# One group of four PSUM buffers for table fills, K generator, DFT steps and transposes of x

## The chip, the core and the metric

The kernel runs on one core of a Trainium2 chip. The metric is the time of one execution in microseconds (us) on the device. A time of the kernel is the median of several runs; the profile is of one further execution.

Engines are called by the names of the profile: PE multiplies matrices (PEld loads its weights), ACT evaluates functions and copies, DVE does elementwise work and copies, POOL sets constants and issues a few transfers, SP issues most transfers. PE writes only into PSUM, which has eight banks of 2 KB for each of its 128 partitions. What PE leaves there has to be copied out ("evicted") by ACT or DVE before the buffer can be filled again.

## The reference, cut to what matters

Two independent halves share the launch: part A, a local attention with 32 heads over x, and part B, a long convolution of u with a kernel K that is generated from parameters.

```python
# part A: qkv = x @ wqkv; each position attends to 8 positions at distance 0, 2, ..., 14
# x (1, 2048, 640), wqkv (640, 1920), wo (640, 640); H = 32, Dh = 20
logits = jnp.einsum("bhsd,bhswd->bhsw", q, kg) * scale
attn = softmax(logits)
a = einsum("bhsw,bhswd->bhsd", attn, vg) -> (1, 2048, 640) @ wo
# part B: u (1, 2048, 640), parameters (640, 192)
P = jnp.exp(logdA[:, :, None] * l[None, None, :])       # l = 0 .. 2047
K = jnp.einsum("dn,dnl,dn->dl", Cc, P, dB).real         # 640 channels x 2048
y = irfft(rfft(K padded) * rfft(u padded))[:2048] + u * Dskip
return concatenate([a, y], axis=-1)
```

## The kernel before, in words

**Part B** works on five chunks (`NCH`) of 128 channels, each in two halves (`th` = 0, 1). A half makes a table of exponentials times sines and cosines, from which the K generator multiplies out K.

- `table_steps` (L185) returns 18 steps for a half. Each takes a PSUM buffer of two banks (`new`, L209), fills it on PE by `block` (L201: matmul lines L203 and L206) and evicts it on ACT: one step for `E` (L216, Exp), three for `M` (L224, Exp), two for `MX` (L238, Exp), twelve for the sines of `Y` and `X` (L252, Sin). Between Exp and Sin, ACT loads a function table. The sines come in three blocks; after the second sine of `Y` in a block DVE does L258, L259 and L260, after the second of `X` it does L264. `M`, `MX` and `E` have one buffer each in SBUF: the next half's L224 waits for this half's L260, L238 for L264.
- `kgen_steps` (L274) is the K generator of a half: 256 small matmuls. L290 reads the first two blocks of `X` and `Y`, L294 reads the third. `jp` = 0 and 1 are two groups of eight channels with one PSUM bank each; each is evicted by one ACT copy (L297) into `Ksb`.
- `fwd_steps` (L366) is a DFT in two rounds of four steps: `f1` (L381, eviction into `A`) and `f2` (L392, eviction into `Ssp`). Every `f2` step reads what all four `f1` steps left in `A`. It is done for u (with `WU`, stored to DRAM as `Udram`) and for K (with `WK`); after each `f2` of K comes a product with the spectrum of u on DVE (`prod`, L420). `inv_steps` holds the first inverse round (`ia`, L429, eviction into `Z`, stored as `Zdram`).
- `Evac` (L337; its copies stand at L342) deals evictions out to engines by a pattern: "d" is DVE, "a" is ACT. For u and `ia` it is "da"; for K it is "d" for `f1` and "aad" for `f2`, and in the last chunk "da" and "a".

`partB` (L437) interleaves the 18 fills of the next half with a list `work`: the K generator of the half just filled, and then either the `ia` steps of the chunk before and the DFT of u of the chunk after next (while `th` = 1 is filled), or the DFT of K of this chunk with its products (while the next chunk's `th` = 0 is filled). In the last chunk `att.transposes` (L628) takes the place of the DFT of u: it transposes x on PE (L637) in 12 steps, evicted into `xa` and `xb`. Then come the projections of q and k (L657), interleaved with what is left of part B, and part A goes on to its products (L713).

PSUM is divided by tags. Before the change: tag "tb", two buffers of two banks, for table fills; tag "k", two buffers of one bank, for the K generator, later for the projections; tag "w", one buffer of two banks, for everything else (`f1`, `f2`, `ia`, transposes). In the last chunk the DFT steps take turns between "w" and "tb".

The order in which instructions stand on each engine is not written out by hand: a scheduler places them at build time, by program order, by what is ready and by free buffers in its own reckoning. Each engine then runs its list strictly in order; a waiting instruction holds up all that stand behind it on its engine. ACT's fills, and in the first chunk some copies, are kept in program order by `InOrder` (L28), so that there are few table loads. SP's queue is also in order.

Of the kernel before, what the change touches and what calls it, by code (L numbers as in the profile page):

```python
# [14 lines left out]
f32 = mybir.dt.float32  # L15
# [22 lines left out]
def params_src(prm):  # L38

    names = ["B_B_re", "B_B_im", "B_C_re", "B_C_im", "B_A_re", "B_A_im"]  # L40
    views = [prm[nm].rearrange("(g c t) n -> c g t n", g=4, c=NCH, t=32) for nm in names]
    return lambda a, c: views[a][c]
# [100 lines left out]
def new_pieces(tc, pools):  # L143


    nc = tc.nc
    PF = pools["arena"].tile([128, 8, CW], f16, name="PF", tag="PF", bufs=2)
    PM = pools["arena"].tile([128, 8, CW], f16, name="PM", tag="PM", bufs=2)
    nc.gpsimd.memset(PF[32:64], 0.0)
    nc.gpsimd.memset(PF[32:33], 4096.0)  # L150
    nc.gpsimd.memset(PM[64:128], 0.0)
    return PF, PM


def load_pieces(tc, P, scr, c, parts, sorder=lambda x: None):
    nc = tc.nc
    PF, PM = P
    where = {0: [(1, PM, 0), (4, PM, 1), (0, PF, 0), (3, PF, 1), (2, PF, 4), (5, PF, 5)], 1: [(6, PM, 2), (7, PM, 3)], 2: [(8, PF, 6), (9, PF, 7)]}
    for p in parts:
        for k, t, r in where[p]:  # L160
            sorder(nc.sync.dma_start(out=t[16 * r:16 * r + 16], in_=scr[c, k].rearrange("(g t) n -> t g n", t=16)))
# [23 lines left out]
def table_steps(tc, pools, R, P, th, order, Y, X, rows=(128, 128), vorder=None):  # L185
# [4 lines left out]
    nc = tc.nc  # L190
# [4 lines left out]
    pool, psp = pools["arena"], pools["psum"]  # L195
# [11 lines left out]
                   tile_position=(0, 64 * h), skip_group_check=True)  # L207

    def new():  # L209
        return psp.tile([128, 2, 512], f32, name="ps_t", tag="tb", bufs=2)  # L210

    def gens():
        ps = new()
        for blk in range(6):
            block(ps[:, 0, 32 * blk:32 * blk + 32], blk, PM, RM[:, 768:800], rows[0])
        order(nc.scalar.activation(out=E[:].rearrange("p k (b q) t -> p b k (q t)", b=6), in_=ps[:, 0, 0:192].rearrange("p (b k t) -> p b k t", k=2, t=16), func=ACT.Exp))  # L216
# [57 lines left out]
def kgen_steps(tc, pools, th, Y, X, Ksb):  # L274
    nc = tc.nc
    MM = nc.tensor.matmul
    st = {}

    def part(jp, half, k0):
        def run():  # L280
            if half == 0 and k0 == 0:
                st[jp] = pools["psum"].tile([128, 8, 64], f32, name="ps_k", tag="k", bufs=2)
            ps = st[jp]
            for k in range(k0, k0 + 4):
                t = 8 * jp + k
                for r in range(2):
                    for g in range(4):
                        o = ps[32 * g:32 * g + 32, k, :]
                        if half == 0:
                            MM(o, lhsT=X[:, r, 4 * g + t // 4, :, t % 4], rhs=Y[:, r, 4 * g + t // 4, :, t % 4], start=(k == 0 and r == 0), stop=False, tile_position=(0, 32 * g), skip_group_check=True)  # L290
                        else:
                            hb = 64 * (g // 2)
                            kq = 4 * (4 + g % 2) + t // 4
                            MM(o, lhsT=X[hb:hb + 64, r, kq, :, t % 4], rhs=Y[hb:hb + 64, r, kq, :, t % 4], start=False, stop=(r == 1),  # L294
                               tile_position=(hb, 32 * g), skip_group_check=True)
            if half == 1 and k0 == 4:
                nc.scalar.copy(out=Ksb[:, 16 * th + 8 * jp:16 * th + 8 * jp + 8], in_=ps[:])  # L297
        return run
    return [part(jp, half, k0) for jp in range(2) for half in range(2) for k0 in (0, 4)]


def fft_consts_np():
# [44 lines left out]
def interleave(a, b):  # L347
    na, nb = len(a), len(b)
    ia = ib = 0
    while ia < na or ib < nb:  # L350
        if ib >= nb or (ia < na and ia * nb <= ib * na):
            a[ia](); ia += 1
        else:
            b[ib](); ib += 1
# [47 lines left out]
def inv_steps(tc, pools, IA, Ud, banks, ev, done):  # L402


    nc = tc.nc
    pool = pools["arena"]
    MM = nc.tensor.matmul
    st = {}

    def load():  # L410
        U = st["U"] = pool.tile([128, 2, 4, 32, 32], bf16, name="U", tag="U")
        fl = lambda t: t.rearrange("p g k t -> p (g k t)")
        nc.sync.dma_start(out=fl(U[:, 0]), in_=Ud)
        for h in range(2):
            nc.sync.dma_start(out=fl(U[64 * h:64 * h + 64, 1]), in_=Ud[64 - 64 * h:128 - 64 * h])

    def prod(S, q):
        ks = slice(8 * q, 8 * q + 8)
        u = st["U"][:, :, :, ks]
        nc.vector.tensor_tensor(out=u, in0=u, in1=S[:, :, ks].unsqueeze(1).to_broadcast([128, 2, 4, 8, 32]), op=A.mult)  # L420

    def ia(q):
        def run():
            if q == 0:
                st["Z"] = pool.tile([128, 128, 32], bf16, name="Z", tag="Z")[:]
            ps = banks("ps_ia")
            for i in range(8):
                for r in range(2):
                    MM(ps[:, i], lhsT=st["U"][:, r, :, :, 8 * q + i].rearrange("p g k -> p (g k)"), rhs=IA[:, r], start=(i % 4 == 0 and r == 0), stop=(r == 1), skip_group_check=True)  # L429
            ev(st["Z"][:, :, 8 * q:8 * q + 8], ps[:].rearrange("p t m -> p m t"))  # L430
            if q == 3:
                done(st["Z"])
        return run
    return load, prod, [ia(q) for q in range(4)]


def partB(tc, pools, prm, B_u, B_Dskip, out_b, att):  # L437
    nc = tc.nc
# [3 lines left out]
    with ExitStack() as outer:  # L442
# [1 line left out]
        Ud = dpool.tile([NCH, 128, 4096], bf16, name="Udram")  # L444
        Zd = dpool.tile([NCH, 128, 4096], bf16, name="Zdram")
        scr = dpool.tile([NCH, 10, 128, CW], f16, name="scr")
        psk = outer.enter_context(tc.tile_pool(name="psum_k", bufs=2, space=bass.MemoryType.PSUM))
        ar = pools["arena"]
        pools.update(psum=psk)
        order, vorder, sorder = InOrder(tc), InOrder(tc), InOrder(tc)  # L450
        tiny = ar.tile([128, 1], f32, name="tiny")
        nc.vector.memset(tiny[:], 1e-36)
        pools["tiny"] = tiny
        tags = [("w", 1)]
        psrc = params_src(prm)
        last = NCH - 1
        ev = Evac(nc, "da")
# [59 lines left out]
        def u_steps(c, ev=ev):  # L517
            return fwd_steps(tc, pools, BD, WU, (lambda t: u[:, :, 32 * c + t]), Banks(psk, tags), ev, ev,
                             done=(lambda S: nc.sync.dma_start(out=Ud[c], in_=S[:].rearrange("p g k t -> p (g k t)"))))
        work = u_steps(0, Evac(nc, "da", dict(a=order, d=vorder)))  # L520
# [8 lines left out]
        for c in range(NCH):  # L529
            Ksb = ar.tile([128, 32, 64], bf16, name="Ksb", tag="Ksb", bufs=2)  # L530
            if c:
                P = nextP
            tg = tags if c < last else [("w", 1), ("tb", 2), ("tb", 2)]
            done = lambda Z, c=c: nc.sync.dma_start(out=Zd[c], in_=Z.rearrange("p m t -> p (m t)"))
            load, prod, ia = inv_steps(tc, pools, IA, Ud[c], Banks(psk, tg), evz, done)
            for th in range(2):
                if c or th:
                    interleave(table_steps(tc, pools, (RF, RM), P, th, order, Yb[th], Xb[th]), work)
                work = kgen_steps(tc, pools, th, Yb[th], Xb[th], Ksb)
                if th == 0:  # L540
                    work += prev_ia if c else []
                    if c + 2 < NCH:
                        work += u_steps(c + 2)
                    elif c + 2 == NCH:
                        work.append(lambda: nc.vector.tensor_tensor(out=u[:], in0=u[:], in1=Dsb[:].unsqueeze(1).to_broadcast([128, 64, 160]), op=A.mult))
                    else:
                        att.load_x()
                        work += att.transposes(lambda: psk.tile([128, 2, 512], f32, name="ps_xt", tag="w", bufs=1))
                    if c < last:
                        nextP = new_pieces(tc, pools)  # L550
                        load_pieces(tc, nextP, scr, c + 1, (0, 1, 2))
                else:
                    load()
                    e2 = Evac(nc, "aad") if c < last else Evac(nc, "a")
                    work += fwd_steps(tc, pools, BD, WK, (lambda t, Ksb=Ksb: Ksb[:, t, :]), Banks(psk, tg), Evac(nc, "d" if c < last else "da"), e2, each=prod)
            prev_ia = ia
        for st in work[:8]:
            st()
        att.load_w()
        kbank = lambda: psk.tile([128, 512], f32, name="ps_qk", tag="k", bufs=2)  # L560
        evh = Evac(nc, "a")
        interleave(work[8:] + prev_ia, att.proj_k(0, kbank, evh) + att.proj_q(0, kbank, evh))
    psa = pools["open_psum_a"]()
# [269 lines left out]
def kernel(  # L833
# [26 lines left out]
    pools["open_psum_a"] = lambda: ctx.enter_context(tc.tile_pool(name="psum_a", bufs=8, space=bass.MemoryType.PSUM))  # L860
    att = Attention(tc, pools, A_x, A_wqkv, A_wo, out_a)
    partB(tc, pools, prm, B_u, B_Dskip, out_b, att)


# [28 lines left out]
```

## Time and profile before

| what | us |
|---|---|
| median of 3 runs (lowest, highest) | 539.57 (536.38, 543.05) |
| the profiled execution's own time | 537.3 |
| span of the profiled execution, first to last instruction | 535.5 |
| PE, DVE, ACT busy, of the span | 396.6, 388.8, 345.6 |

The profiled execution has 1.8 us around its span, and lies 2.27 us below the median.

How to read it: each row of a group has the source line, the engine and operation, the tile written and the tiles read, partitions and elements, how often, the busy time and the mean of one. "Idle before" is how long the engine stood still before these instructions, and the arrow names what ended the wait; "issue" means that the profile shows nothing that it waited for. Rows of the timeline begin with their start in the span. Rows of the stretches begin with the stretch and its length, then busy time and count for PE, PEld, DVE, ACT and POOL, the granted share of PE's clock, the share of the transfer engines and GB/s.

The stages can be told by the first L224 of each half on ACT. They start at 79.2, 119.9, 149.8, 175.5, 205.5, 231.2, 258.6, 282.0 and 315.1 us. These nine stretches are called H1 to H9 here; odd ones fill `th` = 1, even ones `th` = 0 of the next chunk. H1 still contains the preparation of four chunks' parameters on DVE and ACT. After H9's fills come the projections, and at 384.0 us the first product of part A (L713).

### The profile page before, as it was taken

Reading aid. Unit: us, or ns where it says so; the run is one execution under the profiler, and the core shown is the slowest. Engines: PE = TensorE matmul, PEld = TensorE weight load, DVE = VectorE, ACT = ScalarE, POOL = GpSimd, SP = SyncE. Lnnn points to the kernel's source line nnn. Section 1 sums busy time; section 2 is a strip of 40 time slices with the busy share of each in tenths; the row PEclk is TensorE's granted clock in tenths of the full one; section 3 lists DMA queues with packets and bytes.
Section 4 is the critical chain, followed back from the end, with each engine's and each line's share of the span. In section 5 each row is a group of like instructions: output and inputs, shape, how many; then the busy total and the mean of one; then the engine's idle time right before and its main releaser. Section 6 shows DMA issues by size and latency. Waiting matters only on the chain. (4 is left out here: it accounts for less than half of the span.)

```text
span 535.5 us, 15509 instructions
## 1 busy us (share of the span) xinstructions
PE 396.6 (74%) x7009; PEld 253.5 (47%) x7009; DVE 388.8 (73%) x420; ACT 345.6 (65%) x461; POOL 35.5 (7%) x51
## 2 busy tenths in 40 slices
PE   0143778578778967887886787599799797877787
PEld 0012446344556646664554464455444474545345
DVE  3645598795979597989892988434485999985940
ACT  2393486598788987979896869357445273643254
POOL 8700001020012001200000000000000000000000
PEclk9999998598899999999999989999989799776989
DMA  4497133336006400444007008902102003653513
GB/s 123 107 160 190 54 112 121 96 136 138 1 17 190 127 24 18 135 118 148 4 14 225 2 4 287 268 2 80 80 1 62 1 4 82 217 101 109 121 64 111
DMA packets 51706, 51.57 MB, mean 96 GB/s; under 512 B 37416, under 2 KB 48360, under 8 KB 48696
## 3 DMA queue, kind: packets, MB, share of 16 engines
q1 hardware_dynamic: 49752, 49.69, 34.2%
q0 software_dynamic: 1184, 0.89, 0.8%
q8 instruction: 55, 0.90, 0.7%
q10 hardware_dynamic: 704, 0.00, 0.1%
q14 instruction: 11, 0.09, 0.1%
HBM read 32.30 MB, written 18.19 MB: 94 GB/s over the span
## 5 line engine op out<-in xcount | busy, mean ns | idle before, releaser
L252 ACT ACTIVATE X<-ps_t 128x1024 bf16<-128x1024 int16 x60 | 60.2, 1050 | 3.2 <-PE ps_t L203 2.1
L252 ACT ACTIVATE Y<-ps_t 128x1024 bf16<-128x1024 int16 x60 | 59.5, 1040 | 1.7 <-PE ps_t L206 0.9
L203 PE MATMUL ps_t<-R,PF 128*128 128x512 f16 (+1 forms) x160 | 52.3, 422 | 7.1 <-ACT Y L252 3.8
L772 DVE TENSOR_TENSOR prod<-v,attn 128x2048 bf16<-128x2048 bf16 (+1 forms) x48 | 47.6, 1041 | 12.8 <-PE ps_o L776 12.7
L203 PE MATMUL ps_t<-R,PM 128*128 128x256 f16 (+3 forms) x160 | 23.4, 266 | 37.9 <-DMA PM<-scr 23.6
L342 DVE CAST A<-ps_f 128x1024 bf16<-128x1024 f32 x28 | 34.2, 1221 | 23.7 <-PE ps_f L381 23.7
L713 DVE TENSOR_TENSOR prod<-qT,kT 128x5120 bf16<-128x5120 bf16 x16 | 44.6, 2818 | 8.9 <-ACT qT L342 4.7
L342 ACT CAST Ssp<-ps_f 128x1024 bf16<-128x1024 f32 x26 | 26.5, 1020 | 27.5 <-PE ps_f L392 23.9
L258 DVE TENSOR_TENSOR Y<-Y,M 128x2048 bf16<-128x2048 bf16 x30 | 36.6, 1218 | 6.9 <-ACT Y L252 6.9
L260 DVE TENSOR_TENSOR Y<-Y,M 128x2048 bf16<-128x2048 bf16 x30 | 36.6, 1220 | 0.3
L264 DVE TENSOR_TENSOR X<-X,MX 128x2048 bf16<-128x2048 bf16 x30 | 36.6, 1219 | 0.4 <-ACT X L252 0.2
L381 PE MATMUL ps_f<-BD,u 128*64 128x128 bf16 x320 | 22.6, 296 | 17.8 <-DMA BD<-c_BD 6.8
L290 PE MATMUL ps_k<-Y,X 128*32 128x64 bf16 x1280 | 31.4, 240 | 4.8 <-issue 2.8
L203 PEld LDWEIGHTS <-PM 128*128 128x128 f16 (+1 forms) x160 | 13.3, 101 | 44.7 <-DMA PM<-scr 23.6
L776 PE MATMUL ps_o<-prod,ident 32*32 32x512 bf16 (+1 forms) x768 | 23.6, 392 | 13.8 <-DVE prod L772 11.3
L294 PE MATMUL ps_k<-Y,X 64*32 64x64 bf16 x1280 | 27.7, 234 | 5.4 <-issue 3.8
L224 ACT ACTIVATE M<-ps_t 128x1024 bf16<-128x1024 f32 x30 | 29.5, 1033 | 3.3 <-DVE Y L260 1.9
L206 PE MATMUL ps_t<-R,PF 128*64 128x512 f16 (+1 forms) x160 | 26.4, 388 | 6.8 <-ACT Y L252 4.0
L381 PEld LDWEIGHTS <-u 128*64 128x64 bf16 x320 | 21.2, 203 | 21.6 <-issue 20.9
L290 PEld LDWEIGHTS <-X 128*32 128x32 bf16 x1280 | 22.7, 118 | 17.3 <-issue 10.4
L420 DVE TENSOR_TENSOR U<-U,Ssp 128x2048 bf16<-128x2048 bf16 x20 | 23.9, 1221 | 7.3 <-ACT Ssp L342 7.3
L429 PE MATMUL ps_ia<-IA,U 128*128 128x128 bf16 x320 | 25.3, 227 | 4.7 <-DVE Z L342 3.7
(146 smaller groups left out, 794.8 us busy)
## 6 DMA issues: line engine op xcount, KB each, us to landing
Udram<-Ssp SPq DMA_DIRECT2D x5, 1024.0 KB
U<-Udram SPq DMA_DIRECT2D x5, 1024.0 KB
U<-Udram SPq DMA_DIRECT2D x10, 512.0 KB
Zdram<-Z SPq DMA_DIRECT2D x5, 1024.0 KB
zq<-Zdram SPq DMA_DIRECT2D x25, 192.0 KB
u<-in_B_u_dram SPq DMA_DIRECT2D x4, 640.0 KB
xn<-in_A_x_dram SPq DMA_DIRECT2D x4, 640.0 KB
out_dram<-ob SPq DMA_DIRECT2D x16, 160.0 KB
```

The costliest lines, as they stand in the source:

```text
L203: MM(ps, lhsT=Pt[0:K, 2 * blk + th, 0:128], rhs=rhs[0:K], start=True, stop=True, skip_group_check=True)
L224: order(nc.scalar.activation(out=M[:].rearrange("p (q y) -> p q y", q=2)[:, :, 1024 * b:1024 * b + 1024].rearrange("p q (k z) -> p q k z", ...
L252: order(nc.scalar.activation(out=dst, in_=ps[:].bitcast(i16)[:, :, 0::2].rearrange("p i (k z) -> p (i k) z", z=128), func=ACT.Sin, scale=S ...
L258: V.tensor_tensor(out=hi, in0=lo, in1=m(0), op=A.mult)
L260: V.tensor_tensor(out=lo, in0=lo, in1=m(1), op=A.mult)
L264: V.tensor_tensor(out=xf, in0=xf, in1=mx, op=A.mult)
L290: MM(o, lhsT=X[:, r, 4 * g + t // 4, :, t % 4], rhs=Y[:, r, 4 * g + t // 4, :, t % 4], start=(k == 0 and r == 0), stop=False, tile_positio ...
L294: MM(o, lhsT=X[hb:hb + 64, r, kq, :, t % 4], rhs=Y[hb:hb + 64, r, kq, :, t % 4], start=False, stop=(r == 1), tile_position=(hb, 32 * g), s ...
L342: ins = self.nc.scalar.copy(out=out, in_=in_) if e == "a" else self.nc.vector.tensor_copy(out=out, in_=in_)
L381: MM(ps[64 * r:64 * r + 64, i], lhsT=src_fn(8 * q + i), rhs=BD[:, r], start=(i % 4 == 0), stop=True, skip_group_check=True, tile_position= ...
L713: self.nc.vector.tensor_tensor(out=pr[:], in0=self.qT[:, hf], in1=self.kT[:, hf, :, :, HALO - DIL * w:HALO - DIL * w + 256], op=A.mult)
L772: nc.vector.tensor_tensor(out=p2[:, 0:nd], in0=self.v2[b][:, :, off:off + 256], in1=self.attn[:, hf, w, :].unsqueeze(1).to_broadcast([128, ...
```

## The change: what it does

All users of PSUM in part B draw from one tag "b" with four buffers of two banks. The K generator takes one of these for all sixteen channels of a half instead of two of one bank for eight channels each; its eight steps run over both groups of channels for the first two blocks first, then over both for the third, and one ACT copy of 128x1024 takes the place of two of 128x512. The last chunk's DFT has the same four buffers as all others, and so have the transposes and the first projections (which use one bank of each).

```diff
     def new():
-        return psp.tile([128, 2, 512], f32, name="ps_t", tag="tb", bufs=2)
+        return psp.tile([128, 2, 512], f32, name="ps_t", tag="b", bufs=4)
...
-            if half == 0 and k0 == 0:
-                st[jp] = pools["psum"].tile([128, 8, 64], f32, name="ps_k", tag="k", bufs=2)
-            ps = st[jp]
+            if jp == half == k0 == 0:
+                st[0] = pools["psum"].tile([128, 16, 64], f32, name="ps_k", tag="b", bufs=4)
+            ps = st[0]
             for k in range(k0, k0 + 4):
                 t = 8 * jp + k
                 for r in range(2):
                     for g in range(4):
-                        o = ps[32 * g:32 * g + 32, k, :]
+                        o = ps[32 * g:32 * g + 32, t, :]
...
-            if half == 1 and k0 == 4:
-                nc.scalar.copy(out=Ksb[:, 16 * th + 8 * jp:16 * th + 8 * jp + 8], in_=ps[:])
+            if jp == half == 1 and k0 == 4:
+                nc.scalar.copy(out=Ksb[:, 16 * th:16 * th + 16], in_=ps[:])
         return run
-    return [part(jp, half, k0) for jp in range(2) for half in range(2) for k0 in (0, 4)]
+    return [part(jp, half, k0) for half in range(2) for jp in range(2) for k0 in (0, 4)]
...
-        psk = outer.enter_context(tc.tile_pool(name="psum_k", bufs=2, space=bass.MemoryType.PSUM))
+        psk = outer.enter_context(tc.tile_pool(name="psum_k", bufs=4, space=bass.MemoryType.PSUM))
...
-        tags = [("w", 1)]
+        tags = [("b", 4)]
...
-            tg = tags if c < last else [("w", 1), ("tb", 2), ("tb", 2)]
+            tg = tags
...
-                        work += att.transposes(lambda: psk.tile([128, 2, 512], f32, name="ps_xt", tag="w", bufs=1))
+                        work += att.transposes(lambda: psk.tile([128, 2, 512], f32, name="ps_xt", tag="b", bufs=4))
...
-        kbank = lambda: psk.tile([128, 512], f32, name="ps_qk", tag="k", bufs=2)
+        kbank = lambda: psk.tile([128, 512], f32, name="ps_qk", tag="b", bufs=4)
```

The changed program has the same instructions on PE. On ACT, 10 copies take the place of 20. The scheduler's order differs over most of part B: in the built program of the changed kernel PE takes fills and DFT steps in turn, and the DFT steps of a half are done before the next half's fills begin; before, several of them stood between or behind the next half's fills.

## Prediction

> **What bounds the kernel now.** I read the page's busy times first, then the busy times by stretch, then the timelines of PE, ACT and DVE in the stretches that stand still longest.
>
> ```profile
> span 535.5 us, 15509 instructions
> ...
> PE 396.6 (74%) x7009; PEld 253.5 (47%) x7009; DVE 388.8 (73%) x420; ACT 345.6 (65%) x461; POOL 35.5 (7%) x51
> ...
> DVE  3645598795979597989892988434485999985940
> ACT  2393486598788987979896869357445273643254
> ```
>
> No engine is near the span: all three lose a quarter or more. So the stretches, cut at the starts of H1, H2, H4, H5, H6, H8, H9, the end of H9's sines and the first product of part A:
>
> ```profile
> 79.00:120.00 41.00, 29.07 (x521) 19.05 (x523) 35.11 (x67) 28.57 (x36) 4.12 (x3) 0.79 0.35 112
> ...
> 175.00:205.00 30.00, 23.46 (x511) 15.76 (x509) 24.50 (x25) 24.29 (x28) 0.00 (x0) 1.00 0.21 60
> 205.00:231.00 26.00, 22.09 (x400) 16.60 (x403) 22.32 (x22) 23.38 (x27) 4.12 (x3) 1.00 0.41 117
> ...
> 282.00:315.00 33.00, 23.13 (x501) 14.74 (x500) 22.52 (x23) 22.75 (x25) 0.00 (x0) 0.90 0.27 83
> ```
>
> In H1 (79 to 120) DVE is busy 35 of 41 us, with PE's clock at 0.79; in H4 (175 to 205) each engine is busy about 24 of 30 us; H5 (205 to 231) is nearly full; in H8 (282 to 315) each is busy 23 of 33 us. So the loss is not in capacity but in who waits for whom, and it lies in H1 and in the even halves. PE in H1:
>
> ```profile
> 94.13 1.18 PE L381 MATMUL ps_f<-BD,u 128*64 128x128 bf16 x16 [2.03 <-DVE A L342]
> 96.46 1.16 PE L381 MATMUL ps_f<-BD,u 128*64 128x128 bf16 x16 [1.15 <-ACT A L342]
> 98.94 1.18 PE L381 MATMUL ps_f<-BD,u 128*64 128x128 bf16 x16 [1.32 <-DVE A L342]
> 101.23 1.01 PE L392 MATMUL ps_f<-A,WU 128*128 128x128 bf16 x8 [1.10 <-ACT A L342]
> 104.26 1.01 PE L392 MATMUL ps_f<-A,WU 128*128 128x128 bf16 x8 [2.02 <-DVE Ssp L342]
> ```
>
> Five DFT steps in a row, each waiting for the eviction of the one before: one "w" buffer makes a step cost 2.4 us (96.46 to 98.94) where the matmuls take 1.2. ACT at the end of H4 shows where the same chain lands:
>
> ```profile
> 197.11 0.33 ACT L216 ACTIVATE E<-ps_t 128x192 bf16<-128x192 f32 x1
> 198.40 1.01 ACT L342 CAST Ssp<-ps_f 128x1024 bf16<-128x1024 f32 x1 [0.96 <-ACT E L216]
> 200.11 1.01 ACT L342 CAST Ssp<-ps_f 128x1024 bf16<-128x1024 f32 x1 [0.69 <-PE ps_f L392]
> 204.54 1.01 ACT L342 CAST Ssp<-ps_f 128x1024 bf16<-128x1024 f32 x1 [3.42 <-PE ps_f L392]
> 205.45 1.03 ACT L224 ACTIVATE M<-ps_t 128x1024 bf16<-128x1024 f32 x1
> ```
>
> The three late f2 evictions stand in front of M on ACT, so M starts at 205.45, although DVE's L260, which M must wait for, was done at 204.98. DVE in that place:
>
> ```profile
> 202.29 0.42 DVE L259 TENSOR_SCALAR Y<-Y 128x1024 bf16<-128x1024 bf16 x1
> 202.63 1.22 DVE L342 CAST Ssp<-ps_f 128x1024 bf16<-128x1024 f32 x1
> 203.76 1.22 DVE L260 TENSOR_TENSOR Y<-Y,M 128x2048 bf16<-128x2048 bf16 x1
> 204.90 2.35 DVE L420 TENSOR_TENSOR U<-U,Ssp 128x2048 bf16<-128x2048 bf16 x2
> 208.84 1.83 DVE L229 TENSOR_TENSOR M<-M,E 128x1536 bf16<-128x1536 bf16 x2 [1.59 <-ACT M L224]
> ```
>
> Here DVE has no gaps: starts lie 1.13 to 1.14 us apart for casts and products alike (L259 takes 0.34), and DVE is the bound from the first L258 of a half to its end.
>
> **The change part by part.** All spans below run from one half's first M to the next, against the profiled execution's 537.3 us.
>
> *H1, 40.7 us.* With four buffers an f1 step costs its 1.17 us of matmuls, not 2.4. From 46 to 107 us DVE stood idle for PE's f rows by 1.44, 3.51, 2.44, 3.22, 0.80 and 1.75 us: 13.2. Walking the new order with these durations, some 5 stay: the first f2 could start at 52 but its weights WU, asked for at 47.7, land up to 3 us later (the transfer engines are full until 54), and the second f2 round waits some 2 for its last A cast on DVE. That leaves 8; 1 goes to hand-overs. Four casts of the later DFT (4 x 1.13) move into the stage of sines, where DVE has room for some. I take -7; bounds -2 (only the casts leave the chain) and -11 (all but two of these idle us go).
>
> *Even halves, 29.9, 30.0, 27.4 and 33.1 us.* All DFT steps of u now come before the half, so M no longer waits for f2 evictions, and ACT goes from M through two MX and the table load to two sines: 2.8 + 1.5 + 1.3 + 1.9 = 7.5 us after M's start DVE can begin L258. Then DVE has 9 long products, 5 casts and 4 U products at 1.135 and 3 short ones at 0.34: 20.4 + 1.0 = 21.4. M of the next half needs L260, behind which only one U and one X product stand: 7.5 + 21.4 - 2.3 = 26.7. The new wait inside: PE's first f2 stands before a fill of sines and waits for the fourth A cast, about 17 us into the half; behind it on PE all fills wait, and ACT stands still for about 4 us. That is hidden as long as DVE has work, which it has (X of the second block, then U). With 0.8 for hand-overs (the gaps after a release are 0.3 each) 27.5, four times: 110.0 against 120.3, so -10.3. Bounds: -13.5 with no hand-overs, and 0, the DVE-bound H5 being the row that says how much a better order can fail to bring.
>
> *Odd halves H3, H5 (25.7 each), H7 (23.4).* They lose. In the built order 220 of the generator's 256 matmuls stand in one piece, after the last MX fill and before the first sine. That fill needs M's release, so the piece begins about when DVE ends the old half, 2.3 us after M's start. Matmuls of L290 and L294 come every 18.5 ns (79 in 1.42 us): 4.1 us, then fill 0.55, sine 0.95, the Ksb copy 0.95, sine 0.95, and Z stands first on DVE: L258 begins 10.1 us after M. DVE then has 11.2 of products and 5 casts, 16.9: 27.0. With 0.6 for hand-overs 27.6 twice. H7 has no DFT of u, and its piece is 156 matmuls: ACT is its bound with 12 sines at 0.915, M, MX, two loads, Ksb and two Z, 21 us, taken as 22.6 with waits. Sum 77.8 against 74.8: +3. Bounds 0 (the fill comes while PE still multiplies) and +9 (3 us of the piece bare in each).
>
> *The wide copy.* Ten of 128x1024 for twenty at 0.61 us: ACT's casts of that shape take 1.02, so 2.0 us of ACT's time go. It lies beside DVE's chain; were ACT the bound, it would be worth -0.2 a half. Nothing counted.
>
> *End, H9's M to L713, 68.9 us.* The 12 transposes ran through one buffer and waited in the tail (5.54 and 4.10 us in single waits of DVE and ACT); now they stand among H9's sines. H9 pays: the generator's 252 matmuls in one piece, two Z casts ahead of L258, six more casts: DVE ends about 4.7 us later. The generator then ends some 31 us after M, against 34.7 (349.7), and 3.7 us of transposes, projections and f1 are already done: -7.4, less 1.4 for hand-overs, -6. Bounds 0 (H9 pays it all back) and -9 (H9 pays 3).
>
> *Queues.* The store of Udram now stands ahead of six PF loads on SP, and POOL's PM and PF memsets wait for PE's last reads as before (137.4 us of waiting); these tiles are for the chunk after next, some 25 us away, so nothing. If a store held them longer than that, the sines of an even half would wait.
>
> *Instruction supply.* At 287.90 PE stopped 3.82 us for nothing that the profile shows ("issue"), in the generator, while transfers ran at full share; the clock then read 0.79. The new long pieces could meet that more often: 0 to 3.82 an even half; I take 0 net, since H8's own stop may go or stay.
>
> Sum: -7 - 10.3 + 3 - 6 = -20.3, 517.0 us beside 537.3. The median of the runs lies 2.3 above the profiled execution: 519.
>
> [...] The row first: with steps rotating through "tb" buffers the clock was granted at 1.00 from 150 to 282 us, and it fell to 0.50 only from 97 to 106, where the single buffer makes gaps of 1 to 2 us. [...]
>
> **The rivals.** (1) Slower: starved sines. Fills and DFT steps alternate on PE in one ring of three (the fourth is the generator's), and DVE's casts release late, behind products of 1.13 us each. If PE then waits for DVE at each of the 5 or 6 DVE casts of a half, ACT's 24.5 us grow by about 6 to 30.5: seven halves H2 to H8 at 30.5 are 213.5 against 195.1, +18.4; with -4 in H1 and -3 at the end 548.7, some 551 as a median. It decides from 2.9 us lost per half (no gain), and from 4.4 it is slower by 2%. For it: f2's wait above. Against: ACT may lag DVE by three buffers, 2.8 us, and DVE has no gap meanwhile. (2) Same: the even halves stay at DVE's pace of before and only move their loss: H1 -7, even 0, odd +6, end -5: 531.3, as a median 534. For it: H5 and H3 are already full, and 13 us of rearranged casts are not removed work. (3) The buffers bring nothing because the in-order list keeps the f chain: only H1's -2 and the transposes' -3: 532.3, 535 as a median. Against: the built order interleaves.
>
> **How the numbers follow.** Forecast 0.62, rival 1 0.16, rivals 2 and 3 0.22 together. The best of all bounds is -11 - 13.5 + 0 - 9, 506 as a median; the worst, -2 + 0 + 9 + 0 = +7, 547. The range 507 to 545 leaves about 0.04 below and 0.13 above; the forecast's own range is 507 to 529. About 2%, 10.8 us, is what a measurement of this kernel can tell from no change: faster 0.62, same 0.24 (rivals 2 and 3 and a little of 1), slower 0.14.
>
> **What would show it.** Right: the f1 rows of H1 without DVE and ACT waits of 1 to 2 us, the start of H2's M near 113 and of H9's near 300; even halves 27 to 28 us, odd ones 27 to 28 with a DVE wait for the first sine; no ACT wait for f2 ahead of M; the last transpose before the last generator. Wrong: ACT waiting on PE fills all through the sines, with PE held by DVE's release; stops marked "issue" in the generator; a clock below 1.0 between 150 and 280 us.

## The result and the profile after

| what | before | after |
|---|---|---|
| median of 20 runs, us | 537.9 (535.42 to 543.05) | 534.52 (530.07 to 538.8) |
| profiled execution, its own time and span | 537.3, 535.5 | 537.6, 535.8 |
| a second profiled execution of the changed kernel | | 533.32, 531.5 |

The ratio after to before is 0.9914, with a 95% interval of 0.9888 to 0.9941: 0.9% faster, less than half of the 2% that counts as a difference. The forecast was 519. The first profiled execution lies 3.1 us above the median, the second 1.2 below; where they differ both are given.

The head of the page of the kernel after, and its busy DVE and ACT by slices:

```profile
span 535.8 us, 15507 instructions
...
PE 391.0 (73%) x7009; PEld 245.8 (46%) x7009; DVE 389.2 (73%) x420; ACT 345.4 (64%) x451; POOL 35.9 (7%) x51
...
DVE  3656997938878596989885977704585999985840
ACT  2393795957889868986998669557345362633254
```

The work and the busy sums are nearly the same as before. The halves, cut at the first M again, are H1, H2, H4, H5 and H8:

```profile
77.20:109.70 32.50, 22.73 (x416) 14.14 (x414) 29.07 (x53) 25.45 (x32) 4.28 (x3) 0.81 0.35 104
109.70:144.40 34.70, 22.83 (x424) 13.12 (x424) 23.11 (x24) 22.57 (x26) 0.00 (x0) 0.80 0.28 56
...
172.90:202.80 29.90, 20.62 (x360) 11.66 (x349) 22.26 (x23) 22.38 (x24) 0.00 (x0) 0.88 0.11 30
202.80:231.50 28.70, 25.65 (x552) 18.83 (x555) 23.93 (x24) 25.61 (x28) 4.28 (x3) 0.89 0.44 136
...
284.10:313.80 29.70, 20.71 (x359) 11.72 (x347) 22.63 (x23) 22.68 (x25) 0.00 (x0) 0.89 0.20 53
```

H1 fell from 40.7 to 32.5, as forecast. H2 rose from 29.9 to 34.7, H4 stayed at 29.9, H5 rose from 25.7 to 28.7, H8 fell from 33.1 to 29.7. In H2, H4 and H8 every engine is still idle for about a quarter or more, so who waits for whom is again the question. In H1 the chain of waits is gone. PE's DFT steps there, in the timeline of the kernel after:

```profile
95.20 1.19 PE L381 MATMUL ps_f<-BD,u 128*64 128x128 bf16 x16
...
96.93 1.11 PE L381 MATMUL ps_f<-BD,u 128*64 128x128 bf16 x16
...
98.51 1.11 PE L381 MATMUL ps_f<-BD,u 128*64 128x128 bf16 x16
...
101.33 0.62 PE L392 MATMUL ps_f<-A,WU 128*128 128x128 bf16 x8 [1.18 <-DVE A L342]
...
102.44 0.62 PE L392 MATMUL ps_f<-A,WU 128*128 128x128 bf16 x8
```

Steps start 1.6 us apart (96.93 to 98.51) with a fill between them, where they were 2.4 apart; one wait of 1.18 is left, for the fourth A. H2, the half after it, shows what is new. First PE, then ACT:

```profile
113.57 0.65 PE L294 MATMUL ps_k<-Y,X 64*32 64x64 bf16 x31
119.12 0.24 PE L294 MATMUL ps_k<-Y,X 64*32 64x64 bf16 x1 [4.90 <-issue]
119.29 0.64 PE L206 MATMUL ps_t<-R,PM 128*64 128x256 f16 x4
```

```profile
109.69 2.85 ACT L224 ACTIVATE M<-ps_t 128x1024 bf16<-128x1024 f32 x3
113.68 1.02 ACT L238 ACTIVATE MX<-ps_t 128x1024 bf16<-128x1024 f32 x1 [1.13 <-PE ps_t L203]
119.97 0.60 ACT L238 ACTIVATE MX<-ps_t 128x512 bf16<-128x512 f32 x1 [5.26 <-PE ps_t L206]
120.58 1.28 ACT L252 ACT_TABLE_LOAD   x1
```

PE stops for 4.90 us inside the K generator and waits for nothing that the profile shows. The fill of the last MX stands behind it, ACT waits 5.26 us for that fill, and the table load and all twelve sines come that much later. In the stretches around it (107 to 114, 114 to 119, 119 to 124), the last three columns are PE's clock, the share of the transfer engines and GB/s:

```profile
107.00:114.00 7.00, 5.35 (x175) 3.92 (x174) 4.80 (x6) 5.84 (x8) 2.31 (x2) 0.76 0.87 248
114.00:119.00 5.00, 0.23 (x15) 0.04 (x3) 0.41 (x1) 0.70 (x1) 0.00 (x0) 0.80 0.95 153
119.00:124.00 5.00, 4.88 (x107) 2.25 (x108) 0.96 (x1) 3.82 (x4) 0.00 (x0) 0.52 0.13 26
```

The transfer engines are busy for 0.87 and 0.95 of the time until 119, and PE starts again as they fall idle. What runs there are the store of Udram, the loads of U and those of PM and PF; SP issued them from 107.25 on (before: from 117.74), because H1 ended its DFT earlier. In the list of waits (us in total, times, longest), PE's waits of the f2 steps for A, and all waits of the new kind in L294 of the generator:

```profile
PE ps_f L392 <- DVE A L342: 23.5, 6, 4.7
...
PE ps_k L294 <- issue: 16.5, 9, 4.9
```

The 16.5 us include 4.90 in H2, 2.31 in H4, 2.34 in H6, 1.59 in H8, 1.07 in H9 and 3.05 in the last piece, at 349.61; H8 has another of 0.84 in L290. Before, such stops in part B came to 9.7 (1.47, 1.29, 3.82, 3.10). The second profile has 4.68, 2.22, 2.25 at the same places in H2, H4 and H6, and 0.27 in place of the 3.05.

### The profile page after: what moved, and what is told of

The parts are those of the page before. It is cut to its first block, busy times and chain, and to the rows that moved or that the text cites. A ratio compares the mean times of both kernels' runs of the same rounds, so it can differ in the third digit from the quotient of the medians.

```text
span 535.8 us, 15507 instructions
## 1 busy us (share of the span) xinstructions
PE 391.0 (73%) x7009; PEld 245.8 (46%) x7009; DVE 389.2 (73%) x420; ACT 345.4 (64%) x451; POOL 35.9 (7%) x51
## 4 chain that ended last, share of the span: by engine, by line
DVE 36%; PE 34%; ACT 15%; issue 10%; DMA 4%; ACTq 0%; SPq 0%; POOL 0%; DVEq 0%; POOLq 0%
PE ps_qk L657 6%; DVE A L342 4%; DVE Y L258 4%; PE ps_t L203 4%; PE ps_k L290 4%; DVE X L264 3%; DVE prod L772 3%; PE ps_k L294 3%; DVE Y L260 3%; ACT Y L252 3%; PE ps_op L790 3%; PE ps_ia L429 2%; ACT X L252 2%; DVE Ssp L342 2%; DVE prod L713 2%
## 5 line engine op out<-in xcount | busy, mean ns | idle before, releaser
L252 ACT ACTIVATE X<-ps_t 128x1024 bf16<-128x1024 int16 x60 | 61.5, 1055 | 4.8 <-PE ps_t L203 3.3
L252 ACT ACTIVATE Y<-ps_t 128x1024 bf16<-128x1024 int16 x60 | 61.0, 1045 | 5.5 <-PE ps_t L203 3.5
L713 DVE TENSOR_TENSOR prod<-qT,kT 128x5120 bf16<-128x5120 bf16 x16 | 44.6, 2817 | 9.1 <-ACT qT L342 4.7
L203 PE MATMUL ps_t<-R,PM 128*128 128x256 f16 (+3 forms) x160 | 22.9, 272 | 36.5 <-DMA PM<-scr 23.5
L258 DVE TENSOR_TENSOR Y<-Y,M 128x2048 bf16<-128x2048 bf16 x30 | 36.6, 1220 | 15.4 <-ACT Y L252 15.4
L294 PE MATMUL ps_k<-Y,X 64*32 64x64 bf16 x1280 | 26.5, 235 | 16.5 <-issue 16.5
L260 DVE TENSOR_TENSOR Y<-Y,M 128x2048 bf16<-128x2048 bf16 x30 | 36.6, 1218 | 0.2
L381 PE MATMUL ps_f<-BD,u 128*64 128x128 bf16 x320 | 21.8, 290 | 17.5 <-DMA BD<-c_BD 12.0
L203 PEld LDWEIGHTS <-PM 128*128 128x128 f16 (+1 forms) x160 | 13.9, 102 | 44.4 <-DMA PM<-scr 23.5
L294 PEld LDWEIGHTS <-X 64*32 64x32 bf16 x1280 | 19.9, 116 | 30.1 <-issue 29.5
L381 PEld LDWEIGHTS <-u 128*64 128x64 bf16 x320 | 19.7, 204 | 25.5 <-issue 25.5
L224 ACT ACTIVATE M<-ps_t 128x1024 bf16<-128x1024 f32 x30 | 28.5, 1026 | 3.9 <-DVE Y L260 3.9
L392 PE MATMUL ps_f<-A,WK 128*128 128x128 bf16 x160 | 16.5, 265 | 18.2 <-DVE A L342 18.2
L290 PE MATMUL ps_k<-Y,X 128*32 128x64 bf16 x1280 | 24.4, 242 | 5.7 <-ACT Ssp L342 1.9
```

The lines of the kernel that those rows point to most:

```text
L203: MM(ps, lhsT=Pt[0:K, 2 * blk + th, 0:128], rhs=rhs[0:K], start=True, stop=True, skip_group_check=True)
L252: order(nc.scalar.activation(out=dst, in_=ps[:].bitcast(i16)[:, :, 0::2].rearrange("p i (k z) -> p (i k) z", z=128), func=ACT.Sin, scale=S ...
L258: V.tensor_tensor(out=hi, in0=lo, in1=m(0), op=A.mult)
L260: V.tensor_tensor(out=lo, in0=lo, in1=m(1), op=A.mult)
L381: MM(ps[64 * r:64 * r + 64, i], lhsT=src_fn(8 * q + i), rhs=BD[:, r], start=(i % 4 == 0), stop=True, skip_group_check=True, tile_position= ...
L713: self.nc.vector.tensor_tensor(out=pr[:], in0=self.qT[:, hf], in1=self.kT[:, hf, :, :, HALO - DIL * w:HALO - DIL * w + 256], op=A.mult)
```

## The experiments

The theory: the shared buffers do what the prediction said of H1, but the stores and loads that follow a DFT now run under the generator's pieces, and there PE's instructions come late (the supply theory). Rivals: the piece of sixteen channels in one buffer of the ring costs it; the f2 step that waits for the fourth A cast costs it (23.5 us in the list above). Lengths of halves are taken from the starts of M, in the profile of each kernel. Ratios are to the kernel before, run on the same chip.

**hold: the transfers wait for the generator.** `held` stands at the stores of Udram of chunks 2 to 4, at the first load of U of chunk 0, at the loads of PF and PM from chunk 2 on, and at wq and wv. PE's order is nearly as it was.

```diff
-                nc.scalar.copy(out=Ksb[:, 16 * th:16 * th + 16], in_=ps[:])
+                pools["kc"] = nc.scalar.copy(out=Ksb[:, 16 * th:16 * th + 16], in_=ps[:]).ins
...
+def held(tc, pools, ins):
+    tc.add_manual_dep(ins.ins, pools["kc"].name, mybir.DependencyInfo(mybir.DependencyClass.Sync, mybir.DependencyReason.DATA), reason="held")
...
+                    if c < last - 1:
+                        work.append(lambda c=c: held(tc, pools, store(late.pop(), c + 2)))
```

> The changed kernel with the same order on PE, ACT and DVE (20 of 14020 rows differ on PE), but its stores of Udram, the loads of U in chunk 0, the loads of PF and PM and those of wq and wv are made to wait for the generator's copy Ksb of that half, so that no transfer runs under a generator's piece of H2, H4, H6 and the last one. Supply theory (PE's stops marked issue, 16.5 us in L294, are instructions that come late because transfers fill the transfer engines, and 4.9 + 1.8 + 2.1 + 3.0 of them lie on the path): H2 34.7 to about 30, H4 and H6 to about 28, the end 3 shorter, median 522 to 527 against 534.5 for the changed kernel. Rival (the stops are the long pieces' own, or hidden): stops stay, within 2 us of 534.5; or the late loads cost more than they free: slower than 534.5, with waits of U products or sines for DMA.

Measured: 526.54 (523.06 to 529.38), ratio 0.979 (0.9729 to 0.9852). H2 30.5, H4 27.7, H6 28.1, against 34.7, 29.9 and 30.1. PE at the same instruction of H2, in the timeline of this kernel:

```profile
113.67 0.66 PE L294 MATMUL ps_k<-Y,X 64*32 64x64 bf16 x31
114.48 0.23 PE L294 MATMUL ps_k<-Y,X 64*32 64x64 bf16 x1 [0.15 <-issue]
114.63 0.41 PE L206 MATMUL ps_t<-R,PM 128*64 128x256 f16 x4
```

The stop of 4.90 is 0.15; those of H4 and H6 are 0.3 or less. H8 keeps one of 2.19 (see the last section). Against the changed kernel the ratio is 0.979 / 0.9914 = 0.987 (about 0.981 to 0.994, from both intervals). So transfers under the generator cause the long stops of H2, H4 and H6, and these are on the path. The order on the engines hardly differs (20 of 14020 rows of PE's built list; 6 of 451 instructions on ACT and 19 of 420 on DVE in the two traces), so it is the transfers' time that does it.

**f1da: K's f1 casts dealt to DVE and ACT.** PE's order is the same row for row.

```diff
-                    work += fwd_steps(..., Evac(nc, "d" if c < last else "da"), e2, each=prod)
+                    work += fwd_steps(..., Evac(nc, "da"), e2, each=prod)
```

> The changed kernel with the same order on PE; the f1 evictions of K go to DVE and ACT in turn in all chunks (before: DVE alone in chunks 0 to 3). If DVE is the bound of the even halves from the first L258 on, as the prediction said, two casts of 1.135 us less on DVE shorten each of H2, H4, H6, H8 by about 2.3: median 525 to 528. If PE's wait for the fourth A cast (4.5 us) with the fills behind it is the bound, the wait falls to about 2 and the halves shorten by 2 to 3 as well, but DVE then shows gaps. If both are hidden behind the stops of PE and the order of ACT: 533 to 537.

Measured: 523.62 (520.02 to 527.48), ratio 0.9753 (0.9683 to 0.9822). H2, H4, H6, H8 are 32.1, 27.2, 27.0, 28.4, shorter by 2.6, 2.7, 3.0 and 1.3 than in the changed kernel; in H8 a stop of 2.56 takes a part back. PE's wait for the fourth A fell from 4.5 to 1.23. In H4, the changed kernel's wait of PE and what DVE lost by it, then PE's wait in this kernel:

```profile
192.52 1.03 PE L392 MATMUL ps_f<-A,WK 128*128 128x128 bf16 x8 [4.51 <-DVE A L342]
...
196.59 1.22 DVE L420 TENSOR_TENSOR U<-U,Ssp 128x2048 bf16<-128x2048 bf16 x1 [0.69 <-ACT Ssp L342]
```

```profile
187.36 0.61 PE L392 MATMUL ps_f<-A,WK 128*128 128x128 bf16 x8 [1.23 <-ACT A L342]
```

From the first L258 to the next M, H4 took 20.2 us and now takes 17.5. Two casts of 1.135 are 2.3 of that, and DVE's idle 0.69, which is gone, is the rest; so most of the gain is DVE's two casts. DVE is the bound from the first L258 on, and the f2 wait was hidden but for 0.69, as the prediction said.

**k8ring and k8own: the old generator.** In k8ring it has two pieces of eight channels in the shared ring; in k8own they have their own two banks, and the ring has three buffers.

```diff
-            if jp == half == k0 == 0:
-                st[0] = pools["psum"].tile([128, 16, 64], f32, name="ps_k", tag="b", bufs=4)
+            if half == 0 and k0 == 0:
+                st[jp] = pools["psum"].tile([128, 8, 64], f32, name="ps_k", tag="b", bufs=4)
...
+    return [part(jp, half, k0) for jp in range(2) for half in range(2) for k0 in (0, 4)]
```

(k8own: tag "k", bufs=2 for the generator and the projections, and bufs=3 for tag "b".)

> The changed kernel with the old generator: two pieces of eight channels, group by group, each in a buffer of the shared ring, two copies of 128x512 a half. Theory that the piece of sixteen channels costs (the odd halves' 220 to 250 matmuls ahead of the sines, one buffer of four held long, and the last copy only after all 252 matmuls): H3, H5 28.5 to about 26, the last generator 2 us earlier, median 526 to 529. Supply theory: the same matmuls take as many instructions, stops stay, 533 to 537; two pieces at once in a ring of four could even make it slower, 536 to 540.

> The old generator with its own two buffers of one bank (also the projections), and a ring of three for fills, DFT steps and transposes. Theory that the generator in the ring costs: odd halves as in the kernel before (25.7), H1 still about 33, median 525 to 529. Supply theory: stops as in the changed kernel, 532 to 537. If the fourth buffer is what H1 lives on: H1 back towards 37, 537.

Measured: k8ring 536.52, ratio 0.998 (0.9948 to 1.0011); k8own 551.5, ratio 1.0251 (1.0185 to 1.0317). In k8ring H3 and H5 are 29.1 and 28.8, no shorter, and the stops are at the same places (4.99, 2.13, 2.19). So the wide piece is no cost; with its one copy and its order of the pieces it is worth some 0.7%, and the intervals of the two kernels do not touch. The two early copies of a half (536.52) are no better than the one late one (534.52). k8own is a miss of all three expectations. The ring of three starves the sines, the mechanism of the prediction's first rival: between 60 and 400 us ACT waits 40 times for a fill of MX, Y or X, 29.0 us in all, against 18 times and 17.6 us in the changed kernel. That these waits are the whole of the loss was not shown. ACT in H2 of k8own:

```profile
128.57 1.02 ACT L252 ACTIVATE Y<-ps_t 128x1024 bf16<-128x1024 int16 x1 [0.35 <-PE ps_t L203]
...
130.28 1.02 ACT L252 ACTIVATE X<-ps_t 128x1024 bf16<-128x1024 int16 x1 [0.68 <-PE ps_t L203]
...
132.56 1.02 ACT L252 ACTIVATE X<-ps_t 128x1024 bf16<-128x1024 int16 x1 [1.26 <-PE ps_t L203]
```

**firstu: only the first DFTs, in the kernel before.** `Banks(psk, tags if c > 2 else [("w", 1), ("tb", 2), ("tb", 2)])` in the steps of u.

> The kernel before, in which only the DFT steps of u of chunks 0, 1 and 2 take turns between w and tb (as its last chunk's DFT does already); all else as before. Theory that the gain of the change is H1's alone, from more buffers for the f steps there: H1 40.7 to about 33, all other halves as before, median 528 to 531. Rival (only a separate fourth buffer frees H1, since three shared ones starve the fills): H1 stays above 38, 535 to 540.

Measured: 539.53, ratio 1.0058 (1.0022 to 1.0093). H1 is 34.6, shorter by 6.1, and yet nothing is won: M of H1 starts 2.1 later, H2 is 32.3 with a stop of 3.78 in L294 at 123.86 (before: 1.47), H3 28.9. The expectation missed. An earlier DFT puts its store and the loads behind it under H2's generator (transfer share 0.94 from 114 to 124), in the old kernel as in the new one. Why H3 grew was not followed up.

**iafirst: the inverse steps ahead of the generator in odd halves.** `work = prev_ia + work` in place of `work += prev_ia`.

> The changed kernel with the four ia steps ahead of the generator's eight in the list of work of the odd halves. Theory of the prediction that 220 to 250 matmuls of the generator ahead of the first sine make the odd halves longer: DVE's first L258 comes about 7.8 us after M instead of 10.4, H3 and H5 28.6 to about 26, H9 loses ACT's wait of 3.8 for Ksb, median 526 to 529. Rival (DVE's idle time there is given back: the casts of Z only move, and the later generator makes the next half's M or MX wait): 533 to 536.

Measured: 563.61, ratio 1.0498 (1.0431 to 1.0565), a plain miss. In the built order ia steps stand ahead of fills of M on PE, and they need U products that DVE does last: PE waits 4.69 us for DVE U before H3, 18.6 in four such waits, and M comes later by as much. H2 is 40.8, H4 36.0. It tells something else. Zdram's store and U's loads, now early, run under the generator's piece of H3, and a stop appears where the other kernels have 0.3 to 0.5: in the timeline, and the transfer share in the two stretches before:

```profile
161.93 0.40 PE L294 MATMUL ps_k<-Y,X 64*32 64x64 bf16 x13 [3.37 <-issue]
```

```profile
158.00:160.00 2.00, 0.56 (x20) 0.29 (x19) 1.22 (x1) 1.63 (x2) 0.00 (x0) 1.00 1.04 426
160.00:162.00 2.00, 0.07 (x8) 0.08 (x12) 1.65 (x2) 0.00 (x0) 0.00 (x0) 1.00 1.05 250
```

In hold the share under that piece (142 to 148) is 0.01. So the supply theory is seen from both sides: take the transfers away and the long stop goes, bring them in and one comes. Whether the odd halves would gain from earlier sines was not decided by this run.

**both, and the same two edits in the kernel before.**

> The held transfers (526.5 alone) and the f1 casts of K dealt to DVE and ACT (523.6 alone) together in the changed kernel. If the stops of PE and DVE's load in the even halves are two separate costs: 534.5 - 8 - 11 = 515 to 517. If the one hides the other: 521 to 524.

> The kernel before with the two edits that took the changed kernel to 513.0: transfers held back until the generator's last copy, and f1 casts of K dealt to DVE and ACT in turn. It prices the change itself with the stops out of the way. If the stops hid what the shared buffers bring: this kernel loses about 4 by the held transfers and 9 by the casts, 525, and the change is then worth 12, over 2%. If the two edits are worth the same here as in the changed kernel (-19 to -21): 517 to 519, and the change is worth what it was, 4 to 5. If its even halves hang on the late f2 steps and not on DVE: 531 to 534, and the change is worth about 20.

Measured: both 513.0 (509.29 to 516.2), ratio 0.9564 (0.9499 to 0.9629); beforeboth 530.12 (528.32 to 531.78), ratio 0.9853 (0.98 to 0.9906). The edits add up in the changed kernel (-8.0 and -10.9 alone, -21.5 together), so they are separate costs. In the kernel before they bring only 1.5%. With both edits the shared buffers are worth 0.9564 / 0.9853 = 0.971 (about 0.962 to 0.979): 17 us, near the 20 that were forecast, but not where the forecast had them. By the starts of M in the two profiles (19.0 us apart), 10.1 lie in the start and H1, 4.6 in the end up to L713 (69.6 to 65.0) and 3.5 behind it; the even halves sum to 103.1 against 103.6, the odd H3, H5 and H7 to 80.5 against 80.8. The expectation that came nearest to 530.12 was right in the number alone: the even halves of the kernel before did shorten by the two edits, from 120.3 to 103.6, and its odd ones grew by 6.0. Two of the even halves of both:

```profile
109.10:135.30 26.20, 20.46 (x420) 12.54 (x421) 19.74 (x21) 23.86 (x27) 0.00 (x0) 0.90 0.34 102
164.10:189.10 25.00, 19.21 (x361) 11.76 (x350) 20.02 (x21) 23.76 (x26) 0.00 (x0) 0.98 0.21 65
```

ACT is now busy for 23.8 of 25 us in H4. The chain that ends last is still DVE's: from H4's first L258 to H5's M DVE has no gap, and that M waits 1.21 us for L260.

**after2: the changed kernel once more.**

> The changed kernel once more, for a second profile. Supply theory: stops of PE in L294 again of 4 to 5 us in H2 and 2 to 2.5 in H4 and H6, since the same transfers run there; the stop of 3.05 at the end, which a kernel with the same order on PE did not show, may be missing, and H9 to L713 is then about 66. If stops were chance: at other places or of other lengths.

Measured: one run, 533.32. The three stops came again (4.68, 2.22, 2.25); at the end 0.27 in place of 3.05, and H9 to L713 is 66.3. So the first profile's end is too long by its own stop.

**uf1, best4, uf1hold: casts into DVE's idle time.** uf1 is both with `work = us[0:4] + work + us[4:]` in H3 and H5 (us: the eight DFT steps of u); best4 also has `work = kf[0:2] + work + kf[2:]` in the even halves (kf: the steps of K); uf1hold is uf1 with U's first load of chunks 1 to 3 held as well.

> The kernel with both edits (513.0), in which the first four DFT steps of u stand ahead of the generator in the list of H3 and H5, so that two casts on DVE and two on ACT fall where DVE stood idle for 3.7 us. If DVE is the bound of the odd halves from the first L258 on: two casts of 1.135 less behind it, H3 and H5 28.9 to about 26.7, median 508 to 510. Rival (as with the ia steps put first: they stand in the ring ahead of fills, and what waits on them delays M or MX): 513 to 518.

> The same as uf1, and the first two f1 steps of K, which need only the first half of Ksb, ahead of the generator of the even halves. One cast on DVE and one on ACT of each even half move to where DVE stands idle: another 1.1 in each of four, 504 to 506 if both moves work; 511 to 518 if PE's longer piece ahead of the first sine takes it back.

> uf1 with the loads of U of chunks 1 to 3 held back behind the generator's copy as well. Supply theory: uf1 shortened H3 from 28.8 to 27.2 but its later Zdram stores and U loads ended at 165 and 222.5, under the generator, whose stops of 2.26 and 3.45 made H4 and H6 longer by 2.6 and 3.0; with the U loads held these two stops shrink to under 1, H4 and H6 go back to about 25, and the median to 508 to 511. Rival (uf1's longer even halves come from its other order on PE and DVE): 513 to 516; or U lands too late and its products wait: over 516.

Measured: uf1 514.96, ratio 0.9592 (0.9538 to 0.9646), no gain over both; best4 517.05, ratio 0.9611 (0.9554 to 0.9668); uf1hold 509.47 (506.42 to 511.35), ratio 0.9467 (0.9398 to 0.9537), the fastest here (0.990 of both, 0.980 to 1.000). In uf1 H3 fell from 28.8 to 27.2, but H4 and H6 rose from 25.0 and 25.2 to 27.6 and 28.2; the rival of uf1 had the number, 513 to 518, for another reason. PE in H6 of uf1, and in H6 of uf1hold:

```profile
220.60 0.59 PE L294 MATMUL ps_k<-Y,X 64*32 64x64 bf16 x25
224.64 0.29 PE L294 MATMUL ps_k<-Y,X 64*32 64x64 bf16 x7 [3.45 <-issue]
```

```profile
220.08 0.59 PE L294 MATMUL ps_k<-Y,X 64*32 64x64 bf16 x25
221.08 0.29 PE L294 MATMUL ps_k<-Y,X 64*32 64x64 bf16 x7 [0.41 <-issue]
```

With U's load out of the way H4 and H6 are 24.9 and 24.5, as expected of the supply theory. best4 missed: against both, start and H1 grew by 5.3 us, and H6 has a stop of 2.79; the cause in H1 was not followed up.

## Why the prediction was wrong, point by point

Differences to the kernel before, up to L713, by the prediction's own terms, in us:

| term | forecast | first profile | second profile | transfers held (hold) |
|---|---|---|---|---|
| before H1 | 0 | -2.0 | -2.3 | -2.0 |
| H1 | -7 | -8.2 | -8.4 | -7.9 |
| H2, H4, H6, H8 | -10.3 | +4.0 | +4.3 | -4.2 |
| H3, H5, H7 | +3 | +4.9 | +4.5 | +4.5 |
| H9's M to L713 | -6 | -0.2 | -2.6 | -3.7 |
| sum | -20.3 | -1.5 | -4.5 | -13.3 |

Of the 18.8 us between the forecast and the first profile, 14.3 lie in the even halves, 5.8 in the end and 1.9 in the odd halves; the start and H1 gained 3.2 more than forecast.

- *H1*: right, in mechanism and size.
- *Odd halves*: right in sign; H3 and H5 took 28.5 and 28.7 for 27.6, H7 22.5 for 22.6. The first sine waits 1.04 for PE in H3, as the prediction named. That the piece of 220 matmuls is the reason was not shown: two pieces (k8ring) change nothing, and iafirst could not tell.
- *Even halves*: this is where the prediction failed, at the step that it called instruction supply and put at "0 net". It had costed a half as 7.5 us from M to the first L258 (ACT's rows) and 20.0 from there to the next M (DVE's rows). Measured, in us:

  | | H2 | H4 | H6 | H8 |
  |---|---|---|---|---|
  | M to first L258, first profile | 14.4 | 9.7 | 9.8 | 8.1 |
  | first L258 to next M, first profile | 20.2 | 20.2 | 20.2 | 21.6 |
  | M to first L258, hold | 9.0 | 7.5 | 7.8 | 7.8 |
  | first L258 to next M, hold | 21.5 | 20.2 | 20.3 | 22.1 |

  The four halves were put at 110.0 together and took 124.4; 12.1 of the 14.4 us too many lie ahead of the first L258, where ACT waits for an MX fill that stands behind PE's stop (5.26 us in H2, 1.81 in H4, 2.13 in H6). With the transfers held, H4 and H6 take 27.7 and 28.1 for 27.5: the two chains were costed rightly, and the stops were missing. H2 still takes 30.5 there, with 1.2 us of ACT's waits for MX fills and a wait of DVE for Ssp of 2.19, and H8 29.9, with its stop of 2.19.
- *What the gain was measured against*: the even halves of before had stops of their own (1.47 in H2, 1.29 in H6, 3.82 in H8), so a part of the -10.3 was theirs. H2 to H8 together were forecast at -7.3 (-10.3 + 3); the first profile has +8.9 (204.1 for 195.1), hold +0.3 (195.4), and both against beforeboth -0.8 (183.6 for 184.4). So the held stops cost nearly 9, and with most stops out no clear gain of the buffers is left in these halves (a stop of about 2 us in H8 stays in hold and in beforeboth); the bound of "0" that the prediction took from the full H5 was near the value. That DVE has the same work in any order fits this, and f1da shows that DVE's load counts there; but no run shows that it is the whole reason.
- *Instruction supply*: the prediction had the stop of H8 before it, named the long pieces as able to "meet that more often", put the bound at 3.82 a half, and then took "0 net, since H8's own stop may go or stay"; its worst sum of +7 leaves that bound out as well. That was the wrong side: 4.9, 2.3, 2.3 and 1.6 in the four halves. In the *queues* step it saw that the store of Udram stands ahead of six PF loads and asked only when those tiles are needed ("so nothing"). When they run, and what runs on PE at that time, was the question.
- *End*: "The generator then ends some 31 us after M" was 37.9 (313.77 to 351.7). DVE's last product ends at 344.2, 30.4 after M; all 252 matmuls come behind it, two times 2.1 us, and between them the stop of 3.05, which is 0.27 in the second profile. The rest of the end is shorter by 3.6, as said (351.7 to 382.4, before 349.7 to 384.0).
- *New f2 wait*: 4.5 to 4.7 us on PE in each even half, hidden but for 0.69 to 0.73 us of DVE. Right; in hold's H2 it was not hidden (2.19).
- *Wide copy*: nothing was counted for it; k8ring puts old against new form at 0.7%, with the order of the pieces in it.
- *Rivals*: rival 2 was the nearest, 534, and its mechanism is what remains once the stops are out: H1 and the end gain, H2 to H8 only move their loss. Its number is luck: its terms were -7, 0, +6 and -5, and the first profile has -10.2 (with the start), +4.0, +4.9 and -0.2. It did not have the stops. Rival 1's starved sines came in k8own's ring of three. Rival 3 is wrong: H1 gained 8.
- *Granted clock*: a clock below 1.0 between 150 and 280 us, a sign that the prediction named for "wrong", came: it fell from 1.00 to 0.88 in H4 and from 1.00 to 0.83 in H6. In both, with the same rotation through the buffers but without the long waits (the f2 wait of H4 is 1.23 there), H4 and H6 show 0.98 and 1.00; so the rotation alone does not explain the fall. In hold, with the f2 wait of 4.50, H4 still shows 0.88. In the changed kernel's H4 the clock is 0.50 from 178.4 to 181.8 and from 192.1 to 195.5, where the waits of 2.31 and 4.51 end (177.85 and 192.52), and 1.00 between. Not every dip has such a wait: from 202.3 to 209.1 it is 0.50 behind waits of 0.48 to 1.22, and that was not followed up. The clock does not make the difference in time: hold is 8 us faster at a mean clock of 0.899 against 0.895. The prediction's row "it fell to 0.50 only from 97 to 106" was read too narrowly: before the change the clock was 0.50 also from 125.0 to 128.4 and from 142.0 to 145.4.
- *Small slips*: 79 matmuls in 1.42 us are 18.0 ns each, not 18.5, and the terms that lead to 10.1 add up to 9.8. The miss does not hang on them.

## What to carry to other kernels

When an edit makes a stage end earlier, look at what its end triggers: here the stores and loads behind the DFT moved under the densest stretch of matmuls, and PE stopped there (4.90 us in H2 at a transfer share of 0.95, 0.15 with the transfers held). A single "issue" stop under full transfer engines in the profile of before (3.82 us in H8) is a price that any edit can multiply; cost it where transfers and dense pieces of small instructions will meet, and hold the transfers back when nothing needs them soon. A ring of buffers and the load of the busiest engine are priced best with most of those stops taken out: the change was worth 0.9% (0.6 to 1.1) as it stood, and 2.9% (2.1 to 3.8) between the two kernels with both edits.

## What the runs showed of the hardware

All long stops lie at fixed places of PE's instruction list. The first two rows give each stop and the number of matmuls that the trace shows before it. The last two belong to the explanation below: how long after PE began the 128 matmuls ahead of the stop the next packet of instructions started, and the share of the transfer engines in that time.

| stop in the changed kernel | H1 | H2 | H3 | H4 | H6 | H8 | H8 | H9 | last piece |
|---|---|---|---|---|---|---|---|---|---|
| us | 0.48 | 4.90 | 0.45 | 2.31 | 2.34 | 0.84 | 1.59 | 1.07 | 3.05 |
| matmuls before it | 475 | 859 | 1370 | 1752 | 2645 | 3410 | 3537 | 3921 | 4304 |
| packet starts after, us | 0.8 | 5.2 | 0.8 | 3.0 | 3.0 | 2.1 | 3.2 | 0.9 | 2.9 |
| transfer share | 0.13 | 0.95 | 0.40 | 0.97 | 0.94 | 0.95 | 0.93 | 0.00 | 0.95 |

The steps between them are 384, 511, 382, 893, 765, 127, 384 and 383: multiples of 128 to within three (some records are missing). Each matmul has a weight load, so 128 matmuls are 256 instructions (7009 matmuls and 7009 weight loads on the page after). In hold, both, uf1 and iafirst, stops lie at the same counts to within three, whatever their lengths (hold: 1370, 3410, 3536, 3920). The list of transfer queues on the page after has one for instructions, on the same engines (packets, MB, share):

```profile
q1 hardware_dynamic: 49752, 49.69, 34.3%
...
q8 instruction: 55, 0.90, 0.7%
```

0.90 MB in 55 packets are 16.4 KB each. They come one for 128 matmuls: the nine stops of the table end behind the 3rd, 6th, 10th, 13th, 20th, 26th, 27th, 30th and 33rd packet of this queue, and the matmuls before each stop are 128 for each of these packets and 80 to 91 more. At all nine the packet started only after PE had begun the 128 matmuls just ahead, by 0.8 to 5.2 us; why none came earlier is not shown.

The list of transfers that is kept with each trace has the start, the length and the size of every packet, also of this queue. In all 14 profiles PE has 85 stops of over 0.25 us marked "issue" between 60 and 400 us, and every one ends 1.2 to 1.7 us after a packet of 16,384 bytes of this queue has ended. In H2 of the changed kernel the packet runs from 116.22 to 117.62 and PE starts again at 119.12; in H4 it runs from 175.24 to 176.25 and PE starts again at 177.85. So PE waits at these places for the next packet; that it brings PE's next 256 instructions is an estimate from the counts above.

How long it waits follows from the last rows of the table. Where the transfer engines were busy for 0.93 or more, the packet started 2.1 to 5.2 us after PE began the 128 matmuls; at the other three stops it started after 0.8 to 0.9. Without transfers the supply can still be too slow: in H9 the packet started after 0.89 us, took 1.18, and PE went on 1.30 later, 3.37 in all, while the 128 matmuls took 2.30; the rest is the stop of 1.07. And a stop can outlast the transfers. In hold H8's second stop, 2.19 us, has a transfer share of 0.01 in it (282 to 284), after 0.88 in the six us before (276 to 282), where the store of Zdram and the loads of U ran, which hold leaves alone. Its packet started 4.0 us after the 128 matmuls had begun, at 281.56, and ended at 282.68; PE went on at 284.04.
